# Reordering the casts, masks, products and bursts of a fused retention and leaky-ReLU kernel

## The chip, the cores and the metric

The kernel runs on one core of one Trainium2 chip. The metric is the device time of one execution in microseconds (us). Times of single instructions and stretches come from one profiled execution; they are counted from the start of its span, which is the time from its first to its last instruction.

## The reference

The inputs q, k and v are [8 batches, 8 heads, 576 positions, 64] in float32, w_in is [512, 2048], w_out is [2048, 512]. Each head h has a decay `gamma[h] = 1 - 2**(-5-h)`.

```python
scores = scale * np.matmul(q, k.transpose(0, 1, 3, 2))
Dmat = np.where(rel >= 0, gamma[:, None, None] ** rel[None, :, :], 0.0)   # rel = pos_q - pos_k
x = matmul(scores * Dmat, v)          # retention: causal, decayed, no softmax
x = x.transpose(0, 2, 1, 3).reshape(4608, 512)
h = x @ w_in                          # first layer
g = np.maximum(0.01 * h, h)           # leaky ReLU
out = g @ w_out                       # second layer, [4608, 512] float32
```

## The kernel before, in words

**Units and groups.** The 4608 tokens are cut into 36 units of 128 tokens (two chunks of 64) and into 9 groups of 512 tokens, four units each. A unit goes through retention and gives its slice of `xT`, the transposed input of the first layer. A group then goes through the first layer (`gt`, after the leaky ReLU) and the second.

**One unit of retention.** `load` (L119) brings k, q and v in as float32 (256 KB each). `cast_k` (L170) is a ScalarE copy to f16; `cast_q` (L174) and `cast_v` (L177) multiply by a decay table on VectorE, or on GpSimd from unit 8 on. q and k are transposed: for units 0 to 7 on TensorE (`transpose_pe`, L190, one PSUM buffer of `acc` for each, copied out by `transposed`, L206), from unit 8 on by a DMA (`transpose_dma`, L181). `scores` (L209) makes 16 products of q and k and 16 of k and v, in one PSUM tile `sc` that has a single buffer. On VectorE, `masks` (L231) gives the masked scores `s16`, and `state` (L242) carries the running state from chunk to chunk. `state_cast` (L270) makes it f16 for the outputs. `st_before` (L278) shows who needs which: chunk 1 of a unit needs the state cast of chunk 0, chunk 0 of the next unit that of chunk 1.

**Two forms of the outputs.** `outputs_acc` (L309) sums the near and the far part in PSUM, in two halves with a drain of TensorE between; `x_copy` (L340, ScalarE) then writes `xT`. `outputs` (L283) writes both parts apart, without the drain; `own` (L353, ScalarE) copies the near part and `add` (L359, VectorE) adds the far part into `xT`. The tile `ot` has one buffer too.

**First layer.** The pieces are `h_half` (L394: 256 tokens, two blocks of 128 features, 8 matmuls of 256 columns), `h_unit` (L399 to L407: 128 tokens, four blocks, 16 matmuls of 128 columns) and `h_block` (L389: 512 tokens, one block). Each is followed by a ScalarE leaky ReLU of 128x512. They and the TensorE transposes share the four buffers of `acc`.

**Second layer.** Group 0 uses the plain product (`wide`, L419, 16 calls of 4 matmuls of 512 columns). All others use `seven` (L469), a seven-product scheme whose extra operands come from `mix_weights` (L440) and `mix` (L455) on VectorE.

**The order is written by hand.** The scheduler is in manual mode (L82): every engine runs its instructions in program order. TensorE, VectorE, ScalarE, GpSimd and the SyncE queue are five lists, and the position of a call sets its place in each list that it touches. There are three stages:

- L558 to L606, the start: weights and units 0 to 7 are queued for loading, mostly on the GpSimd queue; units 0 to 3 go through retention, and `keep_warm` (L546) puts matmuls with no use between, 512 columns each.
- L633 to L679, group 0's first layer with units 4 to 7 in between, then group 1's first layer. w_in is loaded in four quarters; quarter n holds the feature blocks of `h_half` pieces 2n and 2n+1.
- L720 to L748, group 0's second layer and group 1's. A `burst` (L686) is the scores of one unit with the outputs of the one before it; `ahead` (L701) casts a later unit and transposes it by DMA. From L750 on, groups 2 to 8 follow in a loop.

Of the kernel before, what the change touches and what calls it, by code (L numbers as in the profile page):

```python
# [18 lines left out]
def kernel(  # L19
# [9 lines left out]
    nc = tc.nc  # L29
# [89 lines left out]
    def load(u, eng=None, after=None):  # L119
        for x in (1, 0, 2):  # L120
            t = ld_pool.tile([P, H, D], FP, name=f"t32_{x}")
            t32[u, x] = t
            c = 2 * u
            same = c % CB + 1 < CB
            e = eng[x] if isinstance(eng, dict) else eng or nc.sync
            engs = e if isinstance(e, tuple) else (e,)
            n = H // len(engs)
            for j, rows in ((0, P),) if same else ((0, CH), (1, CH)):
                b, w = (c + j) // CB, (c + j) % CB
                for i, e in enumerate(engs):  # L130
                    hs = slice(n * i, n * i + n)
                    d = e.dma_start(  # L132
                        out=t[CH * j : CH * j + rows, hs],
                        in_=(q, k, v)[x][b, hs, CH * w : CH * w + rows, :].rearrange(
                            "h t d -> t h d"
                        ),
                    )
                    if after is not None:
                        behind(d, *after)
                        after = None  # L140
                    last_load[u, x] = d

# [63 lines left out]
    def transposed(u, x, copy):  # L206
        copy(out=qkT[u][:, x], in_=tr[u, x])
# [261 lines left out]
    def seven(g, hooks, last=False):  # L469

        r = {}
        s = sums[g]

        def product(name, lhs, rhs, fresh):
            if fresh:
                r[name] = acc_pool.tile([P, 2, HN], FP, name="acc")
            order = (
                [(f, tb) for tb in range(2) for f in range(HF)]
                if last
                else [(f, tb) for f in range(HF) for tb in range(2)]  # L480
            )
            for n, (f, tb) in enumerate(order):
                nc.tensor.matmul(  # L483
                    out=r[name][:, tb, :],
                    lhsT=lhs[:, f, tb * P : (tb + 1) * P],
                    rhs=rhs[:, f, :],
                    start=fresh and n == 0,
                    stop=f == HF - 1,
                    skip_group_check=True,
                )  # L490

        def keep(name, of, plus=None):
            r[name] = m_pool.tile([P, 2, HN], FP, name=name)
            if plus is None:
                nc.scalar.copy(out=r[name], in_=r[of])  # L495
            else:
                nc.vector.tensor_tensor(out=r[name], in0=r[of], in1=r[plus], op=ADD)

        def give(a, b, of, plus=None, parts=1):
            if ("o", a) not in r:  # L500
                r["o", a] = o_pool.tile([P, 2, DM], FP, name="osb")
            for n in range(parts):
                ts = slice(n * 2 // parts, (n + 1) * 2 // parts)
                to = r["o", a][:, ts, b * HN : (b + 1) * HN]
                if plus is None:
                    nc.scalar.copy(out=to, in_=r[of][:, ts])
                else:
# [12 lines left out]
            if r["n", a] == 2 and not (last and a == 1):  # L520
                store(g, a, r["o", a])

        plan = (
            ("p1", g_part(g, 0, 0), w_part(0, 0), True, lambda: keep("k1", "p1")),
            ("p1", g_part(g, 0, 1), w_part(1, 0), False, lambda: give(0, 0, "p1")),
            ("p6", s[:, 1], w_mix[:, 1], True, lambda: keep("u2", "p6", "k1")),
            ("p5", s[:, 0], w_mix[:, 0], True, lambda: keep("v", "p5", "u2")),
            ("p7", g_part(g, 1, 0), w_mix[:, 2], True, lambda: give(1, 1, "p7", "v")),
            ("p5", g_part(g, 0, 0), w_part(1, 1), False, lambda: give(0, 1, "p5", "u2")),
            (  # L530
                "p7", g_part(g, 1, 1), w_mix[:, 3], False,
                lambda: give(1, 0, "p7", "u2", 2 if last else 1),
            ),
        )
        for n, (name, lhs, rhs, fresh, then) in enumerate(plan):
            product(name, lhs, rhs, fresh)
            then()
            if n == 0:
                mix(g, 3, 0)
                mix(g, 3, 1)  # L540
            for f in hooks.get(n, ()):
                f()
# [14 lines left out]

    keep_warm(7)  # L558
    load(0, {1: nc.sync, 0: (nc.sync, nc.gpsimd), 2: nc.gpsimd})
    for u in range(1, 3):  # L560
        load(u, nc.gpsimd)
    load(3, {1: nc.sync, 0: nc.gpsimd, 2: nc.gpsimd})
    for f in range(3):
        load_w_in(f)
    load(4, nc.gpsimd)
    load_w_in(3)
    for u in range(5, 8):
# [4 lines left out]
    cast_k(0)  # L572
    transpose_pe(0, 1)
    transposed(0, 1, act_copy)
    keep_warm(2)
    cast_q(0, nc.vector)
    cast_v(0, nc.vector)
    transpose_pe(0, 0)
    transposed(0, 0, act_copy)
    keep_warm(2)  # L580
    cast_k(1)
    cast_q(1, nc.vector)
    for u in range(4):
# [24 lines left out]

    def halves(g, *items):
        for a, fb in items:  # L610
            h_half(g, a, fb)

    def casts(u, eng):
        cast_k(u)
        cast_q(u, nc.vector)
        cast_v(u, eng)

    def turn(u, x):
        transpose_pe(u, x)
# [13 lines left out]
    halves(0, (0, 0), (0, 1))  # L633
    finish(3)
    halves(0, (0, 2), (0, 3), (1, 0), (1, 1))
    casts(4, nc.vector)
    halves(0, (1, 2), (1, 3))
# [24 lines left out]
    settle(6)  # L662
    casts(7, nc.vector)
    h_unit(5, 1)
    turn(7, 1)
    halves(1, (0, 4))
    finish(6)
    turn(7, 0)
    halves(1, (0, 5))
    scores(7)  # L670
    settle(7)
    halves(1, (0, 6), (0, 7))
    finish(7)
    load(8, after=(w_out_loads[2],))
    load(9)
    for n in range(4):
        mix_weights(n, 0)
        mix_weights(n, 1)
        halves(1, (1, 2 * n), (1, 2 * n + 1))  # L679

    def mixes(g, *ns):
        for n in ns:
            mix(g, n, 0)
# [30 lines left out]
    def step(u):  # L714
# [2 lines left out]
        ahead(u + 2)  # L717


    at = {  # L720
        0: lambda: (ahead(8), load(10)),
        3: lambda: (ahead(9), load(11)),
        6: lambda: (ahead(10), load(12)),
        9: lambda: (burst(8, False), ahead(11), load(13)),
        12: lambda: mixes(1, 0),
        14: lambda: mixes(1, 1),
    }
    for n in range(16):
        wide(n // 4, n % 4)
        if n in at:  # L730
            at[n]()

    def early(u):
        burst(u)
        if u < 12:
            ahead(u + 3)
            load(u + 5)
# [12 lines left out]
    first = [f for i in range(4) for f in (i, i + HF)]  # L750
    second = [f for i in range(4, 8) for f in (i, i + HF)]
# [46 lines left out]
```

## Time and profile before

| | |
|---|---|
| median of 7 runs | 309.41 us (306.39 to 311.15) |
| the profiled execution: its time, its span | 309.41 us, 307.6 us |
| mean granted TensorE clock | 0.967 of full |
| TensorE busy, share of the span | 289.3 us, 94% |
| VectorE, ScalarE, GpSimd | 168.5, 144.2, 104.3 us |
| units 0 to 3, up to the first matmul of the first layer | to 22.4 us |
| first layer of groups 0 and 1, units 4 to 7 | 22.4 to 69.7 us |
| second layer of groups 0 and 1, units 8 to 12 | 69.7 to 102.0 us |
| groups 2 to 8 | 102.0 to 303.6 us |

How to read it: the span is 1.8 us shorter than the execution's own time. "Busy" of TensorE counts a matmul at half clock as busy too, so a full row doesn't say that the array ran at its speed; the granted clock has a row of its own (tenths of full speed). A line of the timeline gives start, length, engine, line, operation, and in brackets the idle time before it and what ended that.

### The profile page before, as it was taken

To read this page: it belongs to the slowest core of one execution; us is meant where nothing else is said; L and a number is where in the kernel's file an instruction comes from. 1 tells how busy PE (TensorE), PEld (TensorE's weight loads), DVE (VectorE), ACT (ScalarE), POOL (GpSimd) and SP (SyncE) were. 2 spreads that over 40 slices of the span, in tenths; PEclk is the share of its full clock that TensorE was granted. 3 is DMA by queue.
4 is the path that set the end of the run, shared out by engine and by line. 5 is a ranking of instruction groups with operands and counts; after the bars stand their busy time and mean duration, and the time that the engine had idled before them with its cause. 6 is when DMAs were issued, how large, how long until landed. Compare 5 with 4: busy or idle time off the path is not lost.

```text
span 307.6 us, 9356 instructions
## 1 busy us (share of the span) xinstructions
PE 289.3 (94%) x4071; PEld 196.2 (64%) x4071; DVE 168.5 (55%) x291; ACT 144.2 (47%) x254; POOL 104.3 (34%) x125
## 2 busy tenths in 40 slices
PE   6799976799989999999999999999999999999994
PEld 2468865684467547854884587468647854784583
DVE  1853456620798347735863575557457736741342
ACT  4546642444232576167417723762476247406610
POOL 8949504100644333523352433333334333000000
PEclk9769997979999999999999999999999999999999
DMA  7999999005999999997759667966896651003003
GB/s 216 266 217 225 279 188 205 3 2 132 211 209 271 173 321 207 204 261 158 159 129 284 148 149 157 273 139 142 221 217 113 139 173 36 4 10 129 0 0 139
DMA packets 131258, 50.01 MB, mean 163 GB/s; under 512 B 120752, under 2 KB 125488, under 8 KB 131216
## 3 DMA queue, kind: packets, MB, share of 16 engines
q1 hardware_dynamic: 124864, 39.46, 56.6%
q0 software_dynamic: 6064, 9.83, 14.3%
q8 instruction: 32, 0.52, 0.7%
q10 hardware_dynamic: 288, 0.11, 0.1%
q14 instruction: 10, 0.08, 0.1%
HBM read 36.81 MB, written 9.44 MB: 150 GB/s over the span
## 4 chain that ended last, share of the span: by engine, by line
PE 79%; DMA 6%; SPq 4%; issue 3%; DVE 3%; POOL 2%; ACT 2%; DVEq 0%; POOLq 0%; ACTq 0%
PE acc L373 40%; PE acc L483 28%; DMA t<-in_q_dram 3%; PE sc L215 2%; SPq L132 2%; DMA qkT<-qk 2%; PE ot L321 2%; SPq L183 1%; PE acc L200 1%; PE sc L224 1%; PE acc L549 1%; DMA t<-in_v_dram 1%; PE ot L291 1%; PE ot L302 1%; POOL t L132 1%
## 5 line engine op out<-in xcount | busy, mean ns | idle before, releaser
L373 PE MATMUL acc<-xT,w_in 128*128 128x512 f16 (+2 forms) x736 | 133.8, 340 | 1.8 <-ACT xT L341 1.4
L387 ACT ACTIVATE gt<-acc 128x512 f16<-128x512 f32 x144 | 85.7, 597 | 58.8 <-PE acc L373 57.3
L373 PEld LDWEIGHTS <-w_in 128*128 128x128 f16 x736 | 69.9, 101 | 54.9 <-issue 2.1
L483 PEld LDWEIGHTS <-gt 128*128 128x128 f16 x640 | 61.8, 98 | 10.3 <-issue 1.2
L233 DVE TENSOR_TENSOR s<-sc,cs 128x512 f16<-128x512 f32 x36 | 24.7, 685 | 49.2 <-PE sc L224 49.2
L483 PE MATMUL acc<-w_out,gt 128*128 128x256 f16 x384 | 45.9, 273 | 1.2 <-ACT k L495 1.0
L175 POOL TENSOR_TENSOR qk<-t,cs 128x512 f16<-128x512 f32 x28 | 29.4, 1050 | 42.5 <-DMA t<-in_q_dram 40.9
L273 POOL CAST st<-s 128x512 f16<-128x512 f32 x21 | 12.8, 609 | 85.7 <-DVE s L257 55.8
L355 ACT COPY own<-ot 128x512 f32<-128x512 f32 x28 | 16.4, 586 | 35.0 <-PE ot L302 27.5
L179 POOL TENSOR_TENSOR v<-t,cs 128x512 f16<-128x512 f32 x28 | 31.9, 1139 | 0.5 <-DMA t<-in_v_dram 0.5
L172 ACT CAST qk<-t 128x512 f16<-128x512 f32 x36 | 22.3, 620 | 17.8 <-DMA t<-in_k_dram 12.6
L483 PE MATMUL acc<-w_mix,gt 128*128 128x256 f16 x256 | 30.6, 273 | 0.0
L467 DVE TENSOR_TENSOR mix<-gt 128x1024 f16<-128x1024 f16 x16 | 14.2, 891 | 28.8 <-ACT gt L387 28.8
L483 PE MATMUL acc<-w_mix,mix 128*128 128x256 f16 x256 | 29.4, 273 | 0.0
L483 PEld LDWEIGHTS <-mix 128*128 128x128 f16 x256 | 25.0, 98 | 2.9
L257 DVE TENSOR_TENSOR s<-sc,s 128x256 f32<-128x256 f32 x40 | 16.8, 420 | 6.1 <-PE sc L224 5.6
L360 DVE TENSOR_TENSOR xT<-ot,own 128x512 f16<-128x512 f32 x28 | 19.1, 683 | 1.6 <-ACT own L355 1.6
L215 PEld LDWEIGHTS <-qkT 64*64 64x64 f16 x576 | 7.9, 110 | 12.9 <-issue 10.2
L467 DVE TENSOR_TENSOR mix<-mix,gt 128x1024 f16<-128x1024 f16 x16 | 14.8, 932 | 0.5
L508 DVE TENSOR_TENSOR osb<-acc,u 128x512 f32<-128x512 f32 (+1 forms) x17 | 11.0, 655 | 7.5 <-PE acc L483 7.5
L423 PE MATMUL acc<-w_out,gt 128*128 128x512 f16 x64 | 14.2, 380 | 0.0
L276 POOL CAST st<-s 128x256 f16<-128x256 f32 x7 | 3.2, 454 | 30.2 <-DVE s L261 18.7
(52 smaller groups left out, 246.6 us busy)
## 6 DMA issues: line engine op xcount, KB each, us to landing
out_dram<-osb SPq DMA_DIRECT2D x17, 512.0 KB, 4.0
t<-in_k_dram SPq DMA_DIRECT2D x27, 256.0 KB, 3.8
t<-in_q_dram SPq DMA_DIRECT2D x25, 256.0 KB, 4.4
t<-in_v_dram SPq DMA_DIRECT2D x25, 256.0 KB, 4.5
w_in<-in_moe_w_in_dram POOLq DMA_DIRECT2D x8, 256.0 KB, 6.9
w_out<-in_moe_w_out_dram POOLq DMA_DIRECT2D x4, 512.0 KB, 10.1
t<-in_v_dram POOLq DMA_DIRECT2D x7, 256.0 KB, 5.6
t<-in_q_dram POOLq DMA_DIRECT2D x6, 256.0 KB, 5.8
```

The source lines that it names most:

```text
L172: nc.scalar.copy(out=qk16[u][:, 1], in_=t32[u, 1])
L175: eng.tensor_tensor(out=qk16[u][:, 0], in0=t32[u, 0], in1=decay(u, 0), op=MUL)
L179: eng.tensor_tensor(out=v16[u], in0=t32[u, 2], in1=decay(u, 1), op=MUL)
L233: nc.vector.tensor_tensor(out=s16s[u], in0=sc_tiles[u][:, :, 0], in1=mask_sb.unsqueeze(1).unsqueeze(1).to_broadcast([P, 2, NP, CH]), op=MUL,)
L257: nc.vector.tensor_tensor(out=to, in0=st, in1=carry[0], op=ADD)
L355: nc.scalar.copy(out=owns[u], in_=ot_tiles[u][:, :, 0:NP].rearrange("q j c t -> q c j t"))
L360: nc.vector.tensor_tensor(out=x_of(u).rearrange("q (c g) t -> q c g t", g=2), in0=ot_tiles[u][:, :, NP : 2 * NP].rearrange("q g (c j) t -> ...
L373: nc.tensor.matmul(out=hps[:, n, :], lhsT=w_in16[:, c, f * P : (f + 1) * P], rhs=xT[g][:, c, ts], start=(c == 0), stop=(c == NP - 1),)
L387: nc.scalar.activation(out=out, in_=in_, func=mybir.ActivationFunctionType.Lrelu)
L423: nc.tensor.matmul(out=ys[tb], lhsT=g_t[0][:, f, tb * P : (tb + 1) * P], rhs=w_out16[:, f, :], start=(f == 0), stop=(f == NF - 1),)
L467: nc.vector.tensor_tensor(out=z[:, fs], in0=a[:, fs], in1=b[:, fs], op=op)
L483: nc.tensor.matmul(out=r[name][:, tb, :], lhsT=lhs[:, f, tb * P : (tb + 1) * P], rhs=rhs[:, f, :], start=fresh and n == 0, stop=f == HF - ...
```

## The change

In the start, k of unit 1 is loaded by the SyncE queue and k of unit 3 only after it has landed; the GpSimd queue loses one load, and takes the cast of v of unit 3 between the second and the third quarter of w_in. On VectorE, the mask of unit 0 stands ahead of the casts of q and v of unit 1. There are 29 instead of 23 `keep_warm` matmuls. The outputs of unit 0 stand ahead of the q transpose of unit 1, and two pieces of the first layer stand around the outputs of unit 2.

In the first layer, each cast of k stands earlier on ScalarE, ahead of the state cast that it followed, and the state cast of chunk 1 stands behind the unit's outputs. Units 3 to 6 use `outputs`, `own` and `add` (called `finish2`) in place of `outputs_acc` and `x_copy`. Two `h_unit` pieces (units 6 and 7) replace two `h_half` pieces right after the outputs of unit 7. The pieces of group 0 come in another order. `ahead(8)` with `load(10)` and `ahead(9)` with `load(11)` move from group 0's second layer into group 1's first layer.

In the second layers, bursts 8, 9 and 10 stand at pieces 4 and 9 of `wide` and after its end (before: burst 8 at piece 9, burst 9 after the end), and two bursts instead of three stand inside group 1's `seven`. In the last group, the product p6 is placed between the two products of p1.

```diff
-                    if after is not None:
-                        behind(d, *after)
+                    if after is not None and (x in after or not isinstance(after, dict)):
+                        behind(d, *(after[x] if isinstance(after, dict) else after))
                         after = None
...
+        if last:
+            plan = (plan[0], plan[2], plan[1]) + plan[3:]
...
-    for u in range(1, 3):
-        load(u, nc.gpsimd)
-    load(3, {1: nc.sync, 0: nc.gpsimd, 2: nc.gpsimd})
-    for f in range(3):
-        load_w_in(f)
+    load(1, {1: nc.sync, 0: nc.gpsimd, 2: nc.gpsimd})
+    load(2, nc.gpsimd)
+    load(3, {1: nc.sync, 0: nc.gpsimd, 2: nc.gpsimd}, {1: (last_load[1, 1],)})
+    load_w_in(0)
+    load_w_in(1)
+    cast_v(3, nc.gpsimd)
+    load_w_in(2)
     load(4, nc.gpsimd)
...
-    keep_warm(2)
+    keep_warm(3)
...
-    keep_warm(2)
+    keep_warm(3)
     cast_k(1)
-    cast_q(1, nc.vector)
     for u in range(4):
         n = u + 1
         scores(u)
+        if not u:
+            keep_warm(3)
         state(u, 0)
         state_cast(u, dve_copy, (0,))
         masks(u)
-        if n == 1:
+        if not u:
+            cast_q(1, nc.vector)
             cast_v(1, nc.vector)
         state(u, 1)
         if n < 4:
             transpose_pe(n, 1)
+            transposed(n, 1, act_copy)
+            if not u:
+                keep_warm(3)
+                outputs_acc(0)
+                x_copy(0)
+                keep_warm(1)
             transpose_pe(n, 0)
-            transposed(n, 1, act_copy)
             transposed(n, 0, act_copy)
-            keep_warm(3)
+            keep_warm(3 if u == 1 else 2)
         if n < 3:
             cast_k(n + 1)
             cast_q(n + 1, nc.vector)
+        if n < 2:
             cast_v(n + 1, nc.vector)
         state_cast(u, act_copy, (1,))
-        if n < 4:
-            outputs_acc(u)
-            x_copy(u)
-            keep_warm(1)
+        if u == 1:
+            outputs_acc(1)
+            x_copy(1)
+            keep_warm(2)
+        elif u == 2:
+            h_half(0, 0, 0)
+            outputs_acc(2)
+            x_copy(2)
+            h_half(0, 0, 1)
...
         masks(u)
         state(u, 1)
-        state_cast(u, act_copy, (1,))
 
     def finish(u):
         outputs_acc(u)
         x_copy(u)
+        state_cast(u, act_copy, (1,))
+
+    def finish2(u):
+        outputs(u)
+        own(u)
+        add(u)
+
+    halves(0, (0, 2), (0, 3))
+    finish2(3)
+    halves(0, (0, 4), (0, 5), (1, 0))
+    cast_k(4)
+    cast_qv(4)
+    halves(0, (1, 1), (1, 2), (1, 3))
     turn(4, 1)
-    halves(0, (0, 4), (0, 5))
+    halves(0, (1, 4))
     turn(4, 0)
-    halves(0, (1, 4))
-    casts(5, nc.vector)
-    halves(0, (1, 5))
+    halves(0, (1, 5), (0, 6))
+    cast_k(5)
     scores(4)
     settle(4)
-    halves(0, (0, 6), (0, 7))
-    finish(4)
+    cast_qv(5)
+    halves(0, (0, 7), (1, 6))
+    finish2(4)
+    state_cast(4, act_copy, (1,))
     turn(5, 1)
-    halves(0, (1, 6))
+    cast_k(6)
+    halves(0, (1, 7))
     turn(5, 0)
-    halves(0, (1, 7))
     scores(5)
     settle(5)
-    casts(6, nc.vector)
+    cast_qv(6)
     h_unit(4, 0)
     turn(6, 1)
+    cast_k(7)
     h_unit(4, 1)
-    finish(5)
+    finish2(5)
+    state_cast(5, act_copy, (1,))
     turn(6, 0)
     h_unit(5, 0)
     scores(6)
     settle(6)
-    casts(7, nc.vector)
+    cast_qv(7)
...
     halves(1, (0, 6), (0, 7))
     finish(7)
...
+    load(8, after=(w_out_loads[2],))
+    load(9)
+    h_unit(6, 0)
+    mix_weights(0, 0)
+    mix_weights(0, 1)
+    h_unit(7, 0)
+    for n in range(1, 4):
+        mix_weights(n, 0)
+        mix_weights(n, 1)
+        halves(1, (1, 2 * n))
+        if n < 3:
+            ahead(7 + n)
+            load(9 + n)
+        halves(1, (1, 2 * n + 1))
...
     at = {
-        0: lambda: (ahead(8), load(10)),
-        3: lambda: (ahead(9), load(11)),
-        6: lambda: (ahead(10), load(12)),
-        9: lambda: (burst(8, False), ahead(11), load(13)),
-        12: lambda: mixes(1, 0),
-        14: lambda: mixes(1, 1),
+        1: lambda: (ahead(10), load(12)),
+        4: lambda: (burst(8, False), ahead(11), load(13)),
+        9: lambda: early(9),
+        11: lambda: mixes(1, 0),
+        13: lambda: mixes(1, 1),
     }
...
-    early(9)
+    early(10)
     mixes(1, 2)
-    seven(
-        1,
-        {
-            0: [lambda: early(10)],
-            2: [lambda: early(11)],
-            4: [lambda: early(12)],
-        },
-    )
+    seven(1, {0: [lambda: early(11)], 4: [lambda: early(12)]})
```

More of the change, by code (lines that the diff above doesn't have):

```diff
@@ L611, in halves, with cast_qv @@
             h_half(g, a, fb)
-    def casts(u, eng):
-        cast_k(u)
+    def cast_qv(u):
         cast_q(u, nc.vector)
-        cast_v(u, eng)
+        cast_v(u, nc.vector)
     def turn(u, x):
@@ L631, in finish @@
         x_copy(u)
[L633 to L637, printed above, removed]
+        state_cast(u, act_copy, (1,))
[9 more added lines that the diff above has]
+    halves(0, (1, 1), (1, 2), (1, 3))
     turn(4, 1)
-    halves(0, (0, 4), (0, 5))
+    halves(0, (1, 4))
     turn(4, 0)
-    halves(0, (1, 4))
-    casts(5, nc.vector)
-    halves(0, (1, 5))
+    halves(0, (1, 5), (0, 6))
+    cast_k(5)
     scores(4)
     settle(4)
-    halves(0, (0, 6), (0, 7))
-    finish(4)
+    cast_qv(5)
+    halves(0, (0, 7), (1, 6))
+    finish2(4)
+    state_cast(4, act_copy, (1,))
     turn(5, 1)
-    halves(0, (1, 6))
+    cast_k(6)
+    halves(0, (1, 7))
     turn(5, 0)
-    halves(0, (1, 7))
     scores(5)
     settle(5)
-    casts(6, nc.vector)
+    cast_qv(6)
     h_unit(4, 0)
     turn(6, 1)
+    cast_k(7)
     h_unit(4, 1)
-    finish(5)
+    finish2(5)
+    state_cast(5, act_copy, (1,))
     turn(6, 0)
@@ L666 @@
     halves(1, (0, 4))
-    finish(6)
+    finish2(6)
+    state_cast(6, act_copy, (1,))
     turn(7, 0)
@@ L673 @@
     finish(7)
[L674 to L679, printed above, removed]
     def mixes(g, *ns):
@@ L717, in step, with early @@
         ahead(u + 2)
-    at = {
-        0: lambda: (ahead(8), load(10)),
-        3: lambda: (ahead(9), load(11)),
-        6: lambda: (ahead(10), load(12)),
-        9: lambda: (burst(8, False), ahead(11), load(13)),
-        12: lambda: mixes(1, 0),
-        14: lambda: mixes(1, 1),
+    load(8, after=(w_out_loads[2],))
[12 more added lines that the diff above has]
+        halves(1, (1, 2 * n + 1))
+    def early(u, out=True):
+        burst(u, out)
+        if 8 < u < 12:
+            ahead(u + 3)
+            load(u + 5)
+    at = {
+        1: lambda: (ahead(10), load(12)),
[3 more added lines that the diff above has]
+        13: lambda: mixes(1, 1),
     }
@@ L731 @@
             at[n]()
[L733 to L737, printed above, removed]
-    early(9)
-    mixes(1, 2)
-    seven(
-        1,
-        {
-            0: [lambda: early(10)],
-            2: [lambda: early(11)],
-            4: [lambda: early(12)],
-        },
-    )
+    early(10)
+    mixes(1, 2)
+    seven(1, {0: [lambda: early(11)], 4: [lambda: early(12)]})
     first = [f for i in range(4) for f in (i, i + HF)]
```

## The prediction

> **What bounds the kernel now.** I read the page first: TensorE is busy for 94% of the span, and over slices of 7.7 us its granted clock falls below 9 tenths only in slices 2, 3, 7 and 9.
>
> ```profile
> PE 289.3 (94%) x4071; PEld 196.2 (64%) x4071; DVE 168.5 (55%) x291; ACT 144.2 (47%) x254; POOL 104.3 (34%) x125
> PEclk9769997979999999999999999999999999999999
> ```
>
> So TensorE's own list is the bound, and only idle time or half clock on it can be won. The table by stretches says where: from 102 to 276 us TensorE is busy for 173.74 of 174.00 us at full clock, while the change touches nothing there. From 69.7 to 102 it is busy for 29.95 of 32.30. The rest lies before 69.7. The waits of TensorE, longest in total first:
>
> ```profile
> PE acc L200 <- ACT qk L172: 5.0, 4, 2.3
> PE acc L373 <- ACT xT L341: 1.4, 1, 1.4
> ...
> PE sc L215 <- DVE stmp L260: 1.2, 1, 1.2
> ...
> PE acc L483 <- ACT k L495: 1.0, 2, 0.7
> ```
>
> The k transposes wait for ScalarE's k cast. TensorE's timeline places the three long waits of the first layer, and ScalarE's shows what stood before two of the casts:
>
> ```profile
> 43.01 0.40 PE L200 MATMUL acc<-ident,qk 128*128 128x128 f16 x4 [1.87 <-ACT qk L172]
> 51.73 0.60 PE L200 MATMUL acc<-ident,qk 128*128 128x128 f16 x4 [2.34 <-ACT qk L172]
> 61.02 8.81 PE L373 MATMUL acc<-xT,w_in 128*128 128x256 f16 x64 [1.38 <-ACT xT L341]
> ```
> ```profile
> 42.03 0.40 ACT L276 CAST st<-s 128x256 f16<-128x256 f32 x1 [1.63 <-DVE s L257]
> 42.34 0.61 ACT L172 CAST qk<-t 128x512 f16<-128x512 f32 x1
> ```
>
> k of unit 6 had been issued at 26.56 and landed 6.8 us later, at 33.4; its cast waited 9 us behind a state cast. Each wait also brings a stretch of half clock. By stretches:
>
> ```profile
> 44.94:48.36 3.42, 3.29 (x69) 2.80 (x64) 0.42 (x1) 1.08 (x2) 0.00 (x0) 0.50 0.86 182
> 48.36:51.77 3.41, 1.07 (x21) 0.90 (x18) 3.18 (x7) 1.12 (x4) 2.13 (x2) 1.00 0.98 224
> 51.77:55.19 3.42, 3.33 (x44) 2.42 (x44) 1.27 (x2) 0.99 (x2) 2.44 (x3) 0.50 0.40 88
> 62.01:65.42 3.41, 3.41 (x19) 2.41 (x17) 1.50 (x3) 1.19 (x2) 0.00 (x0) 0.50 0.00 0
> ```
>
> First columns: length, TensorE busy; third from the end: clock. Three stretches of 3.41 us at half clock cost up to 1.7 us each. A fourth, 10.81 to 21.05, lies in the start.
>
> [...]switches at 10.81, 21.05, 44.94, 48.36, 51.77, 55.19, 62.01 and 65.42 lie on one grid of 3.413 us. [...]1.38 us of wait in one grid step (58.60 to 62.01, busy 1.95) was enough. [...]v's cast takes 0.69 us alone and 1.53 at 51.18, beside a GpSimd cast of 1.52.
>
> **The change part by part.** I follow TensorE's list through the new order with the old durations at full clock: an `h_half` or `h_unit` piece 0.875 us, four transposes 0.22, scores 0.38, `outputs` 0.37 (84.33 to 84.70), `outputs_acc` 0.8 to 0.9, a `keep_warm` matmul 0.22 (0.43 at half clock). On the others: casts of q and v and masks 0.60 back to back (0.68 alone), state 0.42 or twice that, state casts 0.30 to 0.41, ScalarE's leaky ReLU, `own`, `x_copy` and k cast 0.6, `add` 0.68.
>
> *Start.* I compare at one point: all of units 0 to 3 and six pieces done. Before: `outputs_acc(3)` ends at 25.12, four more pieces would give 28.6. After: v of unit 0 still lands at 7.8, so the first scores end at 8.86. With the mask first, the outputs of unit 0 can run at 10.45 instead of 11.53. At full clock the chain of VectorE and TensorE then puts the scores of units 1, 2 and 3 at 12.5, 16.0 and 20.0 (before 13.1, 17.8, 22.0). Scores of unit 3 end at 20.35; state, cast, mask and state take VectorE 2.3, then ScalarE 0.4 for the state cast, 1.2 for two leaky ReLUs behind it and 0.6 for `own`, VectorE 0.65 for `add`: piece (1,0) starts at 25.5. If the clock stays at half from 10.8 to 21 as now, the six extra fillers cost 0.43 each and the scores of unit 3 end at 25, so (1,0) starts at 30.1. Between them I take 26.5, near the warm end, since the fillers stand where TensorE was idle (its waits sum to 3.3 us between 1.19 and 11.53). Worth -2.1 (from -3.1 to +1.5). The k load that waits on SyncE has only unit 8 behind it, due at 44 us. GpSimd's v cast waits for v (landed at 14.2) and holds back the third quarter of w_in, issued at 12.5 before, to some 15.4. Its two loads landed at 21.7 and 23.0, behind four others still under way, so they should land no later; (0,4) needs them at 22.5 to 23.0. If that cover is gone, it costs 1 us for each us.
>
> *First layer, from (1,0) to the end of the scores of unit 7.* Before: 28.62 to 56.83, 28.2. After, work: 12 `h_half` and 4 `h_unit` pieces 14.0, eight transposes 1.8, four scores 1.5, three `outputs` 1.1, together 18.4. Waits that remain or are new: scores 5 right after its q transpose must await the VectorE copy, 0.6; `own` and `add` of unit 5 come behind a leaky ReLU on ScalarE and two casts and a copy on VectorE, while `h_unit(5,0)` needs the result, 1.45 (before 0.4 behind `x_copy`); q transpose of unit 7 0.45; scores 7 behind `add(6)` and the copy 0.9. Sum 22.0 with rounding. The 1.45 leaves a grid step about 57% busy, so I charge one drop, 1.7: 23.7, worth -4.5 (from -6.2 to -2.8 with none or two). This holds the gain of the k casts: k of units 5, 6 and 7 land at 30.2, 33.4 and 35.6, and ScalarE comes to their casts at about 33, 35.5 and 38.5. All ScalarE instructions behind such a cast would wait with it, then the leaky ReLUs, then the four `acc` buffers.
>
> *From there to the end of group 1's first layer.* Before 12.84 (56.83 to 69.67). After: two pieces 1.75, `outputs_acc(7)` 0.8, two `h_unit` pieces 1.75 that hide `x_copy(7)`, six pieces 5.25: 9.55. The 1.38 wait and its half clock go. Worth -3.3; without that cover it is -0.2.
>
> *Second layers of groups 0 and 1.* Before 32.33. After: 64 matmuls of 512 columns (14.0) and 112 of 256 (12.25), with five bursts of scores and `outputs` (3.3): 29.5. VectorE is the risk: its mixes took 2.97 for two beside GpSimd's casts (1.48 alone), and `mix(1,1)` now ends right at burst 10. I find 1.0 us of wait at burst 11 for `sc` and the state cast, and 0.7 in small ones: 31.2, worth -1.1 (from -2.5 to +0.5). DMA: transposes 8 and 9 with loads 10 and 11 are issued from about 56 us instead of 71, into what was 54 to 72 us of almost no transfer; the DMA engines were busy for all of 72 to 102, so this adds slack.
>
> *Last group.* p6 in place of the wait of 0.72 for the copy k1; its operand is ready at 292.55, p6's fifth matmul would ask at 292.49. Worth -0.6.
>
> Sum: -2.1 - 4.5 - 3.3 - 1.1 - 0.6 = -11.6. The profiled execution's own time is 309.41 (span 307.6, 1.8 around it), equal to the median, so 309.4 - 11.6 = 297.8 us.
>
> **Rivals.** (a) The waits move rather than go: the start stays cold and the `own`/`add` chains bring two or three drops. For it: VectorE now carries `add` four times in the densest stretch (3.18 of 3.41 us busy at 48.36 to 51.77). Against: the new gaps are smaller than 1.87 and 2.34. Time: +1.5, -2.8, -3.3, +0.5, -0.6 is -4.7, 304.7; halfway 301 to 302. (b) All stays warm: -3.1 - 6.2 - 3.3 - 1.7 (without the small waits) - 0.6 = -14.9, 294.5; if the new waits don't come either, 291.5. (c) Slower: GpSimd's queue behind the v cast. All of w_in's second half, units 4 to 7 and w_out are issued behind it. For it: at 13 to 23 us that queue already waits for landings. Against: it has four loads ahead then. At a landing of the third quarter at about 34.5 instead of 23.0 the gain is gone, at 38 the kernel is 1% slower (312.5). (d) It doesn't do what it says: k lands late once casts come early, ScalarE blocks, and the waits return under the name of a DMA; with slacks of 2 to 3 us I expect little: 306 to 309.
>
> **How the numbers follow.** Likeliest 0.50 (294.5 to 300), (a) 0.30 (300 to 305), (b)'s lower part 0.09 (291 to 294.5), (c) 0.04, (d) 0.07. From 292 to 304.5 leaves out about 2 in 10. Faster by over 1% (below 306.3) is the first three with a little of (d): 0.90; within 1% 0.06; slower 0.04. About 1% is what a measurement of this kernel can tell from no change.
>
> **What would show it.** Right: no wait of `acc L200` on `qk L172` over 0.5 us after 30 us; group 2's first block at about 91 us instead of 102.0; 174 us from there to 276's counterpart unchanged; one or two half-clock stretches before 60 us; no wait of 0.7 on L495. Wrong: `h_unit(5,0)` without a wait on `xT` (my 1.45 is too much), w_in landing after 23 us with TensorE waiting on it, half clock up to 21 us again, or waits of ScalarE's L172 on a DMA.

## The result and the profile after

The changed kernel takes 294.64 us (median of 11 runs, 294.08 to 297.51), the kernel before 308.14 us (28 runs, 305.28 to 311.15). The ratio is 0.9586, with a 95% interval of 0.9553 to 0.9619. Medians here take in all runs; ratios leave out the slow ones, which are those over 1.5% above the fastest of the same kernel. The profiled execution took 295.62 us, 1.0 more than the median, with a span of 293.8 us, 13.8 less than the span shown before. My 297.8 was 3.2 us too high: 1.9 in the gain (11.6 forecast, 13.5 by the medians) and 1.3 in the base (309.4 instead of 308.14).

From the page after: TensorE's busy time and its granted clock in slices of 7.3 us.

```profile
PE 281.3 (96%) x4101; PEld 190.9 (65%) x4101; DVE 172.6 (59%) x294; ACT 144.2 (49%) x254; POOL 105.2 (36%) x125
PEclk9999999999999999999999999999999999999999
```

TensorE runs 30 instructions more and is busy 8 us less, and no slice falls under nine tenths of the clock. The waits of TensorE after, longest in total first:

```profile
PE acc L373 <- issue: 1.4, 1, 1.4
PE sc L215 <- DVE qkT L207: 1.3, 2, 0.7
...
PE acc L373 <- DVE xT L360: 1.2, 1, 1.2
PE acc L373 <- ACT qkT L207: 1.0, 1, 1.0
...
PE acc L200 <- ACT qk L172: 0.2, 1, 0.2
```

The 5.0 us behind ScalarE's k casts are down to 0.2. What is new stands in TensorE's timeline:

```profile
17.81 1.03 PE L373 MATMUL acc<-xT,w_in 128*128 128x256 f16 x8 [0.96 <-ACT qkT L207]
23.25 0.94 PE L373 MATMUL acc<-xT,w_in 128*128 128x256 f16 x7
25.61 4.65 PE L373 MATMUL acc<-xT,w_in 128*128 128x256 f16 x41 [1.42 <-issue]
38.10 0.32 PE L215 MATMUL sc<-qkT 64*64 64x64 f16 x16 [0.75 <-DVE qkT L207]
42.55 1.05 PE L373 MATMUL acc<-xT,w_in 128*128 128x128 f16 x16 [1.18 <-DVE xT L360]
```

The first line is put down to a copy that had ended at 17.08; the second load of w_in's first quarter was issued at 9.9 and landed some 7.8 us later, at 17.7; that is the last thing I find which the piece needs. The third is a pause inside a piece: seven matmuls at 23.25, then the eighth 1.42 us later. The last two were foreseen: the copy ahead of the scores of unit 5 (0.6 forecast, 0.75 measured) and `add` ahead of unit 5's piece (1.45 forecast, 1.18 measured). ScalarE shows the k cast of unit 6 behind a state cast again, but this one is ready:

```profile
36.08 0.58 ACT L355 COPY own<-ot 128x512 f32<-128x512 f32 x1
36.55 0.42 ACT L276 CAST st<-s 128x256 f16<-128x256 f32 x1
36.85 0.63 ACT L172 CAST qk<-t 128x512 f16<-128x512 f32 x1
```

Last the stretches (length, busy time of TensorE, its weight loads, VectorE, ScalarE and GpSimd, clock, DMA share, GB/s): end of the first layer, second layers of groups 0 and 1, and the loop.

```profile
49.08:59.03 9.95, 9.78 (x140) 8.64 (x130) 9.31 (x12) 7.08 (x13) 4.84 (x4) 1.00 0.52 118
59.03:89.13 30.10, 29.68 (x466) 19.62 (x464) 21.10 (x33) 9.28 (x16) 14.68 (x15) 1.00 1.04 223
89.13:263.55 174.42, 174.22 (x2563) 115.80 (x2560) 104.69 (x175) 88.18 (x153) 56.19 (x65) 1.00 0.74 164
```

Group 2's first block begins at 89.13 instead of 102.00. From there to the first block of group 8 it takes 174.42 us, where the kernel before took 174.49 (102.00 to 276.49): the loop is as it was. From that block to the end of the span it is 30.25 after and 31.11 before.

### The profile page after: what moved, and what is told of

Same layout as the page of the kernel before. It is cut to its first block, busy times and chain, and to the rows that moved or that the text cites. A ratio compares the mean times of both kernels' runs of the same rounds, so it can differ in the third digit from the quotient of the medians.

```text
span 293.8 us, 9414 instructions
## 1 busy us (share of the span) xinstructions
PE 281.3 (96%) x4101; PEld 190.9 (65%) x4101; DVE 172.6 (59%) x294; ACT 144.2 (49%) x254; POOL 105.2 (36%) x125
## 4 chain that ended last, share of the span: by engine, by line
PE 85%; DVE 7%; issue 2%; POOL 2%; DMA 2%; ACT 1%; DVEq 0%; POOLq 0%
PE acc L373 41%; PE acc L483 33%; PE acc L423 3%; PE sc L215 3%; POOL t L132 2%; DMA t<-in_v_dram 2%; PE sc L224 1%; DVE mix L467 1%; PE ot L291 1%; DVE s L233 1%; PE ot L302 1%; DVE xT L360 1%; DVE s L257 1%; PE ot L321 1%; DVE qkT L207 1%
## 5 line engine op out<-in xcount | busy, mean ns | idle before, releaser
L373 PE MATMUL acc<-xT,w_in 128*128 128x512 f16 (+2 forms) x752 | 130.9, 330 | 3.6 <-issue 1.4
L373 PEld LDWEIGHTS <-w_in 128*128 128x128 f16 x752 | 67.8, 98 | 55.9 <-issue 4.4
L233 DVE TENSOR_TENSOR s<-sc,cs 128x512 f16<-128x512 f32 x36 | 24.7, 686 | 44.0 <-PE sc L224 44.0
L175 POOL TENSOR_TENSOR qk<-t,cs 128x512 f16<-128x512 f32 x28 | 30.1, 1075 | 22.6 <-PE sc L224 14.2
L355 ACT COPY own<-ot 128x512 f32<-128x512 f32 x32 | 18.7, 585 | 38.8 <-PE ot L302 31.6
L179 POOL TENSOR_TENSOR v<-t,cs 128x512 f16<-128x512 f32 x29 | 33.2, 1146 | 4.3 <-DMA t<-in_v_dram 3.5
L467 DVE TENSOR_TENSOR mix<-gt 128x1024 f16<-128x1024 f16 x16 | 14.9, 936 | 28.8 <-ACT gt L387 28.8
L483 PE MATMUL acc<-w_mix,mix 128*128 128x256 f16 x256 | 29.6, 273 | 0.0
L360 DVE TENSOR_TENSOR xT<-ot,own 128x512 f16<-128x512 f32 x32 | 21.9, 684 | 3.0 <-ACT own L355 3.0
L467 DVE TENSOR_TENSOR mix<-mix,gt 128x1024 f16<-128x1024 f16 x16 | 14.0, 879 | 0.5
```

Source lines behind the costliest of these rows:

```text
L175: eng.tensor_tensor(out=qk16[u][:, 0], in0=t32[u, 0], in1=decay(u, 0), op=MUL)
L179: eng.tensor_tensor(out=v16[u], in0=t32[u, 2], in1=decay(u, 1), op=MUL)
L233: nc.vector.tensor_tensor(out=s16s[u], in0=sc_tiles[u][:, :, 0], in1=mask_sb.unsqueeze(1).unsqueeze(1).to_broadcast([P, 2, NP, CH]), op=MUL,)
L355: nc.scalar.copy(out=owns[u], in_=ot_tiles[u][:, :, 0:NP].rearrange("q j c t -> q c j t"))
L360: nc.vector.tensor_tensor(out=x_of(u).rearrange("q (c g) t -> q c g t", g=2), in0=ot_tiles[u][:, :, NP : 2 * NP].rearrange("q g (c j) t -> ...
L373: nc.tensor.matmul(out=hps[:, n, :], lhsT=w_in16[:, c, f * P : (f + 1) * P], rhs=xT[g][:, c, ts], start=(c == 0), stop=(c == NP - 1),)
```

## The experiments

Twelve runs in three sets of four, each set on another chip. The kernel before was timed beside each set; its median was 306.64, 307.54 and 307.90 us. "Changed kernel" stands for the 294.64 above, or for 294.28 in the third set, where it ran again. Differences "more" or "less" are of medians. Across sets they are rough: in the first set the kernel before was faster and its ratios have intervals of up to 0.02, so that fewer fillers, for one, are 0.5 us slower than the changed kernel by the medians and 2.4 by the ratios (0.9665 against 0.9586). Where two sets differ by less than 2 or 3 us, the profiles have to decide.

### The k casts put back

```diff
-    cast_k(5)      # and those of units 6 and 7, from their earlier places
     scores(4)
     settle(4)
+    state_cast(4, act_copy, (1,))      # and those of units 5 and 6
+    cast_k(5)
     cast_qv(5)
...
     finish2(4)
-    state_cast(4, act_copy, (1,))
```

> The changed kernel with the k casts of units 5, 6 and 7 put back behind the state casts of the unit before, and those state casts back ahead of the outputs; all else as changed. Theory (k casts free TensorE's list): the two long waits of the k transposes of units 6 and 7 come back, 1.5 to 2.3 us each, and at least one of them brings a half-clock step of 1.7, so 3.5 to 6 us slower than the changed kernel (ratio to before about 0.97 to 0.978). Rival (VectorE's chain of own, add and casts bounds this stretch anyway, so the waits overlap with those that are there): under 1.5 us slower, ratio under 0.964.

Measured: 300.44 us, ratio 0.9852 (0.9767 to 0.9938), 5.8 us more than the changed kernel. TensorE's timeline and the clock:

```profile
40.12 0.61 PE L200 MATMUL acc<-ident,qk 128*128 128x128 f16 x4 [1.81 <-ACT qk L172]
49.12 0.40 PE L200 MATMUL acc<-ident,qk 128*128 128x128 f16 x4 [2.22 <-ACT qk L172]
```
```profile
PEclk9999978999999999999999999999999999999999
```

Both waits are back, and the clock falls in slices 6 and 7 (some 37 to 52 us), where TensorE waits. The rival falls: VectorE's chain does not hide them. The ratio lies above the expected 0.978; part of that is the faster kernel before of this set.

### The k casts alone

```diff
-    settle(u): ... state(u, 1); state_cast(u, act_copy, (1,))
+    settle(u): ... state(u, 1)          # state cast behind x_copy, units 4 to 7
+    cast_k(5)   # after piece (1,4);  cast_k(6) after turn(5, 1);  cast_k(7) after turn(6, 1)
```

> The kernel before with one edit: the k casts of units 5, 6 and 7 earlier on ScalarE and the state casts of units 4 to 7 behind the outputs. Theory (k casts are the largest single part and stand alone): the waits of 1.87 and 2.34 us go, with one or two half-clock steps, so 4 to 6 us faster than before (ratio 0.980 to 0.987), while the wait of 1.38 for unit 7's copy stays. Rival (they only pay together with the other forms of outputs and the new order): under 2 us, ratio over 0.993.

Measured: 300.26 us, ratio 0.9733 (0.9671 to 0.9795), 7.3 us less than before: more than expected, and over half of the whole gain, from the casts of k and the state casts that change places with them. TensorE's timeline of this kernel:

```profile
52.18 7.15 PE L373 MATMUL acc<-xT,w_in 128*128 128x256 f16 x64 [0.67 <-ACT xT L341]
59.16 8.80 PE L423 MATMUL acc<-w_out,gt 128*128 128x512 f16 x40
...
83.08 0.32 PE L215 MATMUL sc<-qkT 64*64 64x64 f16 x16 [2.15 <-DMA qkT<-qk]
89.38 0.32 PE L215 MATMUL sc<-qkT 64*64 64x64 f16 x16 [1.89 <-DMA qkT<-qk]
93.53 4.48 PE L373 MATMUL acc<-xT,w_in 128*128 128x512 f16 x20
```

The second layer begins at 59.16, where the changed kernel has 59.03: up to there, in these two executions, this edit alone brings as much as all of them. The changed kernel has new waits on this way that the other lacks, 0.96, 1.42 and 1.18 us among them. But the second layers then take 34.4 us (59.16 to 93.53) against 30.1, with 4.0 us of wait for DMA transposes. Whether the earlier k casts cause these waits is not shown: the second profile of the kernel before, further down, has 3.6 us of them although its second layers begin at 65.93.

The clock of this profile reads full throughout, yet its start ran at half clock. Three fillers take 1.49 us at first and 0.81 later:

```profile
PEclk9999999999999999999999999999999999999999
```
```profile
10.38 1.49 PE L549 MATMUL acc<-idle 128*128 128x512 f16 x3
18.49 0.81 PE L549 MATMUL acc<-idle 128*128 128x512 f16 x3
```

Four transposes take 0.61 us at 6.88 too, and 0.39 at 29.16. So the clock of a page, and the mean clock of a run, can miss half clock in the start.

### The old second layers

```diff
-    ahead(8), load(10), ahead(9), load(11) inside group 1's first layer; bursts 8, 9 at pieces 4, 9
-    early(10); ...; seven(1, {0: early(11), 4: early(12)})
+    0: (ahead(8), load(10)), 3: (ahead(9), load(11)), 6: ..., 9: (burst(8, False), ...)
+    early(9); ...; seven(1, {0: early(10), 2: early(11), 4: early(12)})
```

> The changed kernel with the second layers of groups 0 and 1 as before: units 8 and 9 cast and transposed inside group 0's second layer, burst 8 at piece 9, three bursts inside the seven products. Theory: the 2.2 us that this stretch gained (32.3 to 30.1) come back, from waits of VectorE's backlog at the third burst, so 1.7 to 2.5 us slower than the changed kernel. Rival (the loads come earlier now in any case, so the order no longer matters): under 0.7 us.

Measured: 297.93 us, ratio 0.9680 (0.9623 to 0.9737), 3.3 us more than the changed kernel, above the expected range. By landmarks the same: 58.05 to 91.42 is 33.4 us against 30.1. Its three waits:

```profile
80.75 0.32 PE L215 MATMUL sc<-qkT 64*64 64x64 f16 x16 [1.43 <-DVE stmp L260]
81.72 0.32 PE L291 MATMUL ot<-s,v 64*64 64x64 f16 x16 [0.53 <-DVE xT L360]
87.27 0.32 PE L215 MATMUL sc<-qkT 64*64 64x64 f16 x16 [1.50 <-DMA qkT<-qk]
```

The first two are the backlog of VectorE that the kernel before had too (1.2 and 0.5); the third is the transpose of unit 12. The first profile of before had no wait for a transpose there; the second one, shown below with p6 alone, awaited two, 1.41 and 2.23 us, and its second layers took 34.0 us (65.93 to 99.95) instead of 32.3. So the rival falls. The edit puts back both the `ahead` calls and the places of the bursts; what each is worth alone is not shown.

### The start and its fillers

```diff
     # fewer fillers: 2, 2 instead of 3, 3; none behind scores(0) and T(1, k)
     # old start: loads, casts and order of units 0 to 3 as before, pieces (0,0), (0,1) behind
```

> The changed kernel without eight of the filler matmuls of the start (those that the change added ahead of the first first-layer piece: one, one, three and three). Theory (the fillers hold the clock through the start): half clock returns for two or three steps of 3.41 us between 7 and 21 us, the first first-layer piece starts 0.5 to 3 us later than at 17.8 and the kernel is 1 to 3 us slower (ratio 0.962 to 0.969). Rival (the order of casts and masks alone closes the gaps, or w_in's landing at 17.7 sets the first piece in any case): same time within 0.5 us, first piece at 17.8. The pause of 1.42 us inside a piece at 25.6 should stand about 16 TensorE instructions later in the list if it is a fetch of instructions, and at the same instruction if it is a data wait.

> The changed kernel with the whole start of before (loads, casts, fillers, order of units 0 to 3, two first-layer pieces after the start). Theory: the start gives 2 us of the gain, so 2 us slower than the changed kernel (ratio 0.965), with half clock from about 11 to 21 us. Rival (w_in and the loads bound the first layer, so a slow start is caught up): within 0.7 us.

Measured: fewer fillers 295.12 us (ratio 0.9665, 0.9596 to 0.9733), old start 295.76 us (0.9679, 0.9599 to 0.9759): 0.5 and 1.1 us more than the changed kernel. With fewer fillers the clock is at half for two steps, from 9.7 to 16.6 us, and the first piece starts at 18.66 instead of 17.81:

```profile
PEclk9689999999999999999999999999999999999999
```
```profile
18.66 1.04 PE L373 MATMUL acc<-xT,w_in 128*128 128x256 f16 x8
...
24.10 1.92 PE L373 MATMUL acc<-xT,w_in 128*128 128x256 f16 x16
26.82 3.44 PE L373 MATMUL acc<-xT,w_in 128*128 128x256 f16 x30 [0.80 <-DVE xT L360]
```

So without these eight fillers two steps ran at half clock, where the changed kernel's clock was full. But all but 0.2 us of the delay is gone by 26.82, where (1,0) awaits `add(3)`: in the changed kernel (1,0) starts at 26.6, behind the pause. The old start, at half clock from 9.1 to 15.9, gave its first piece at 20.61 and a second layer at 59.32 against 59.03. The forecast of 2 us for the start seemed too large; the third set takes this up. The pause itself is not to be seen with fewer fillers, at no instruction.

### Outputs in the old form

```diff
     def finish2(u):
-        outputs(u); own(u); add(u)
+        outputs_acc(u); x_copy(u)
```

> The changed kernel with outputs_acc and x_copy for units 3 to 6 in place of outputs, own and add. Theory (the form without a drain saves 0.43 us of TensorE four times, but its add costs the wait of 1.18 before unit 5's piece and parts of two others): the two nearly cancel, within 1 us of the changed kernel (ratio 0.956 to 0.962). Rival 1 (the outputs form is a main source of the gain): 1.5 to 3 us slower. Rival 2 (the add chain costs more than it saves): 1 us or more faster.

Measured: 293.90 us, ratio 0.9641 (0.9545 to 0.9737), 0.7 us less than the changed kernel by the medians and 1.7 more by the ratios. The profiles say that the two forms nearly cancel. From the first piece to the second layer it took 40.5 us (17.21 to 57.73), the changed kernel 41.2, of which 0.56 is its longer pause. By the estimate above the form without the drain saves TensorE some 1.7 us (four times 0.43, the difference of 0.8 and 0.37 us in the first profile). It pays them back in waits: 1.18, 0.75, 0.59 and 0.39 us between 37 and 49 us in the changed kernel, where this one has 0.52 and 0.34.

### No cover for unit 7's copy, and p6 alone

```diff
-    h_unit(6, 0); ...; h_unit(7, 0)
+    halves(1, (1, 0)); ...; halves(1, (1, 1))
```

> The changed kernel with the two half pieces right behind unit 7's outputs again, which need unit 7, in place of the two pieces of units 6 and 7. Theory: TensorE waits about 0.9 us for x_copy of unit 7 there; if the wait brings a half-clock step, 2.5 us slower than the changed kernel, if not, 0.9 us. Rival (the wait of before was long because ScalarE's state cast and two leaky ReLUs stood ahead of the copy, and these are gone): under 0.5 us.

Measured: 295.77 us, ratio 0.9600 (0.9545 to 0.9656), 1.1 us more than the changed kernel by the medians, 0.4 by the ratios. The profile shows a wait of 0.67 us for `x_copy` at 52.25, and no half clock. The first theory had the mechanism, with 0.9 for the wait; the time alone cannot tell 0.5 from 0.9.

```diff
+        if last:
+            plan = (plan[0], plan[2], plan[1]) + plan[3:]      # on the kernel before
```

> The kernel before with one edit: p6 between the two products of p1 in the last group. Theory: the wait of 0.72 us for k1 goes and nothing else changes, 0.6 to 0.9 us faster, which is below what the times of this kernel can tell; the profile shows it. Its profile is also a second look at the start and the first layer of before: if the half-clock stretches depend on the phase of the clock's grid, their places and number differ from the first look, while the waits of 1.87, 2.34 and 1.38 stay.

Measured: 306.52 us, ratio 0.9984 (0.9948 to 1.0020), no difference that the times show. From group 2's first block to the end it takes 204.75 us (99.95 to 304.7), the kernel before 205.6, the changed kernel 204.67. The wait for k1 is gone; in its place the 16 matmuls on the mixed weights take 2.04 us instead of 1.91:

```profile
289.93 2.04 PE L483 MATMUL acc<-w_mix,mix 128*128 128x256 f16 x16
291.81 1.91 PE L483 MATMUL acc<-w_out,gt 128*128 128x256 f16 x16
```

This is also a second profile of the start and the first layer of before. Its clock:

```profile
PEclk9599997799999999999999999999999999999999
```

The waits of 1.87 and 2.35 are there as in the first profile; the one of 1.38 is 0.67 here, against the expectation. And half clock runs from 9.1 to 15.9 and from 50.0 to 56.9 (two grid steps each), not from 10.8 to 21.1, 44.9 to 48.4, 51.8 to 55.2 and 62.0 to 65.4, and the span is 304.7 instead of 307.6. So the profile on which I forecast was one with much half clock.

The wait of 1.87 brought none this time. Its grid step and the next one, here:

```profile
39.77:43.18 3.41, 1.89 (x50) 1.69 (x52) 1.99 (x5) 2.02 (x4) 0.00 (x0) 1.00 1.22 199
43.18:46.59 3.41, 2.96 (x82) 2.48 (x74) 1.33 (x4) 1.18 (x2) 0.00 (x0) 1.00 1.10 188
```

TensorE was busy for 1.89 us of that step. In the first profile, steps with 1.84 (41.53 to 44.94) and 1.95 (58.60 to 62.01) were followed by half clock. Nor did half clock follow the transposes' waits of 1.41 and 2.23 here, or those of 2.15 and 1.89 with the k casts alone. So the forecast's "each wait also brings a stretch of half clock" does not hold in general, and these runs do not settle what decides it.

### The start once more, and two attempts at a better kernel

```diff
     # acc and turn:     outputs_acc, x_copy for units 3 to 6; turn(5, 0) ahead of piece (1, 7)
     # w_in first:       and load_w_in(0) ahead of load(3); cast_v(3) behind load_w_in(2)
     # acc, old start:   the first of these, with the whole start of before
     # change again:     the changed kernel, unaltered
```

> The changed kernel with outputs_acc and x_copy for units 3 to 6 (as in the run that had these alone) and the q transpose of unit 5 ahead of the last half piece of group 0, so that its copy is covered. Theory (the waits of TensorE for add and for the copy are all that the new form costs): the waits of 1.18, 0.75 and 0.59 are gone, 1 to 2 us faster than the changed kernel run beside it. Rival (outputs_acc's drain gives it back): within 0.5 us.

> The run with outputs_acc and the earlier transpose, and also the first quarter of w_in ahead of q and v of unit 3 on the GpSimd queue, and GpSimd's cast of v of unit 3 behind the third quarter. Theory (the first piece waits for w_in's landing at 17.7): the first piece starts at about 16.8 and the kernel is another 0.5 to 1 us faster. Rival (unit 3 comes late instead, or the pause inside a piece at about 25 us takes it up): within 0.4 us.

> The changed kernel once more, unaltered, as the measure beside the three others of this call: about 294.6 us, and if the pause of 1.42 us inside a piece of the first layer belongs to the place in TensorE's list, it is there again after the seventh matmul of that piece.

> The run with outputs_acc and the earlier transpose, but with the whole start of before. With the changed kernel's own first layer the old start cost only 0.3 to 1.1 us, while my sum said 2.1. If the waits for add hid the difference, the old start is 1.5 to 2.5 us slower here than the run without it. If the start itself is worth little, because w_in and the pause in the list set the pace of the first pieces, it is under 1 us slower.

Measured in one set: changed kernel again 294.28 us (ratio 0.9577, 0.9534 to 0.9621), acc and turn 293.17 (0.9550, 0.9503 to 0.9597), w_in first 299.03 (0.9651, 0.9582 to 0.9720), acc with the old start 295.98 (0.9657, 0.9599 to 0.9714).

*Acc and turn* is 1.1 us under the changed kernel, at the low end of what I expected; five of its six times (292.49 to 293.71) lie below five of the other's six (293.85 to 294.88), but the intervals of the ratios overlap. It is the best of all kernels here by its median. The waits of 1.18, 0.75 and 0.59 are gone; 0.34 for `x_copy` remains.

*Old start with acc* costs 2.8 us against *acc and turn*, more than I expected, and the intervals of these two just fail to overlap. So by the times the start is worth about what I forecast. Why it is more here than the 1.1 before is argued, not shown: the pause and the late `add(3)` can have hidden a part in the changed kernel. The profiles of these two differ by only 0.7 us of span (292.6 and 291.9), and this execution of the old start ran at full clock from 4.7 us on and was the fastest of its six. What made the others slower, up to 298.52, is not shown.

*W_in first* is slower than *acc and turn* by 0.0101 of the kernel before, some 3 us. The rival is right in kind, unit 3 comes late, and it costs far more than the 0.4 us that it allowed. The page's clock and the lines of TensorE, ScalarE and GpSimd:

```profile
18.65 0.62 PE L200 MATMUL acc<-ident,qk 128*128 128x128 f16 x8 [2.96 <-ACT qk L172]
```
```profile
17.97 0.62 ACT L172 CAST qk<-t 128x512 f16<-128x512 f32 x1 [4.13 <-DMA t<-in_k_dram]
```
```profile
18.24 1.14 POOL L179 TENSOR_TENSOR v<-t,cs 128x512 f16<-128x512 f32 x1 [5.19 <-DMA t<-in_v_dram]
```
```profile
PEclk9987999999999999999999999999999999999999
```

With two loads of w_in ahead of q and v of unit 3, k of unit 3 comes late as well, though it is on the other queue and its issue there had ended at 7.8 us, as in *acc and turn*; how the loads delay it is not shown. Its cast starts at 17.97 instead of 13.97, the k transpose waits 2.96 us, and half clock follows (8 and 7 tenths in the slices from 14.8 to 29.6 us). ScalarE kept to the order of its list, so this is rival (d) of the forecast, at another place: a k cast that waits for its load, with 4.13 us of idle time ahead of it, holds up what stands behind it on ScalarE, here a state cast that ran at 15.30 in *acc and turn* and runs at 18.50.

*The changed kernel again* missed my expectation on the pause. The first piece started at 16.62, as w_in's first quarter landed over a microsecond sooner, and TensorE then waited for w_in's third quarter; no pause followed:

```profile
22.99 5.45 PE L373 MATMUL acc<-xT,w_in 128*128 128x256 f16 x48 [0.85 <-DMA w_in<-in_moe_w_in_dram]
```

## Why the prediction was right, step by step

The time lies in the range, on its low side. The largest step, the k casts, came as forecast and is shown by experiments. In the start and at the end of the first layer the sum is right for another reason, and that is luck. By its own steps (spans, us; the loop gives another -0.1):

| step | forecast | changed kernel's profile | the experiments |
|---|---|---|---|
| start, to piece (1,0) | -2.1 | -2.0 (28.6 to 26.6) | 1.1; 2.8 with the old outputs |
| (1,0) to the scores of unit 7 | -4.5 | -5.7 (28.2 to 22.5) | k casts back: +5.8 |
| to the end of the first layer | -3.3 | -2.9 (12.84 to 9.95) | cover alone: 0.67 of wait |
| second layers of groups 0 and 1 | -1.1 | -2.2 (32.3 to 30.1) | old order: +3.3 |
| last group | -0.6 | -0.9 (31.1 to 30.2) | p6 alone: -0.85 |
| sum | -11.6 | -13.8 | |

**K casts: right, shown from both sides.** Put back they cost 5.8 us, alone they bring 7.3, and the long waits come and go with them.

**The clock: mis-sized.** I charged one half-clock step, 1.7 us, because the wait for `add` would leave a grid step 57% busy, as the step of 58.60 to 62.01 had been (1.95 of 3.41 us), which half clock followed. It did wait, 1.18 us, and no half-clock step followed in any of six profiles with that wait (the changed kernel twice, without cover, the old second layers, fewer fillers, the old start; 1.18 or 1.19 us each). After the first 6 us no half clock came before 290 us, where I had expected one or two stretches before 60. That term is most of what was missing in the second row: 22.0 without it, against 22.5 measured. The other side of it is the kernel before. In 26 of its executions, those beside the first two sets, the mean granted clock runs from 0.956 to 0.997 and the time from 303.56 to 312.27 us; a straight line through them (correlation -0.57) gives 1.4 us for each 0.01 and 304.7 at full clock. From this estimate some 10 us of the gain would be waits and order, and about 3.4 clock. It is a weak estimate: the line explains a third of the spread, the mean clock can miss half clock in the start, and it counts half clock after the last matmul (all that the changed kernel's 0.998 lacks, from 292.84 on). In the two profiled executions TensorE's busy time alone differs by 8.0 us, for 30 instructions more. So the split between clock and waits stays open. The changed kernel's runs have 0.994 to 1.000 and spread by 3.4 us. Half clock in the start differs between the two profiles of before as well: 10.24 us in the first, 6.83 in the second.

**The start: right in size by luck.** I put 26.5 between a warm and a cold chain. The clock stayed full, as in my warm chain (25.5), but w_in's first quarter landed at 17.7 instead of 17.0 as in the profile before (0.96 of wait), and the pause took 1.42; I had neither. In the second execution, without both, (1,0) starts at 24.7, which makes this step -3.9. The cover that I named for w_in's third quarter was as thin as said: in the second execution TensorE waited 0.85 us for it.

**The end of the first layer: right in size, wrong cause.** I gave nearly all of the 3.3 us to the cover of unit 7's copy and said that 0.2 remains without it. Without the cover the stretch takes 10.5 us (48.76 to 59.23) against 9.95 with it, so it is worth some 0.5. The rest of the gain is the half clock and half of the wait of 1.38, and both belonged to one execution: in the second profile of before, without any cover, the wait is 0.67 and no half clock follows it.

**The second layers: right sign, too small.** I foresaw 1.0 us at burst 11 and 0.7 in small waits; one wait of 0.42 came. What I treated as slack was worth more: the old order runs into the DMA transposes in three of its four profiles (1.5 us of wait on the changed kernel, 4.0 with the k casts alone, 3.6 with p6 alone). The gain of this step therefore depends on the others, and on the execution of before that it is held against: 2.2 us against its first profile, 3.9 against its second, 3.3 against the old order on the changed kernel. That VectorE's mixes stretch beside GpSimd's casts came as forecast. A pair of weight mixes took 2.98 us beside them, a pair of the same form 1.28 us with GpSimd idle:

```profile
53.17 2.98 DVE L448 TENSOR_TENSOR w_mix<-w_out,w_mix 128x1024 f16<-128x1024 f16 x2
57.28 1.28 DVE L448 TENSOR_TENSOR w_mix<-w_out,w_mix 128x1024 f16<-128x1024 f16 x2
```

GpSimd cast q and v of unit 9 from 52.84 to 55.60. Nothing waited for these mixes.

**The rivals.** (a), waits that move to `own` and `add`, was true in kind: 0.75, 1.18 and 0.59 us; *acc and turn* shows that they cost about 1 us. (c), GpSimd's queue, did not come in its size: v of unit 3 was cast at 14.11, as its load landed, and the wait for w_in's third quarter was 0 in one execution and 0.85 us in the other. (b), all warm, is what happened, 294.5 in the forecast; that the time agrees to 0.1 us is luck, since its gain of 14.9 was 1.4 too large and its base 1.3 too high.

## What to carry to other kernels

An engine that works through one list for two chains should run the instruction whose input is ready long before first: here three casts, moved past a state cast, were worth half of a 13.5 us gain. When one stage becomes faster, look at what feeds the next: with that edit alone TensorE waited 4.0 us for the transposes behind it. A wait of TensorE can cost more than its length, as half clock may follow (it did after waits of 1.38, 1.87 and 2.34 us in the first profile of before); but it is no fixed charge, since waits of up to 2.23 us passed here without. A profile with half clock is one draw among several, so take a second one before pricing it, and compare the length of like instructions, not the clock row alone.

## What I had not expected

- **A pause inside a piece.** In five profiles (the changed kernel, without cover, old second layers, old outputs, acc and turn) TensorE stops for 0.4 to 1.4 us inside piece (0,4), behind the seventh matmul, or behind the sixth where `outputs_acc` has put one drain more into the list. No data wait is shown. In a sixth (acc with the old start) it stops for 0.64 us at another place, behind seven of eight matmuls of unit 2's outputs (18.94 us). Before that stop 443 matmuls and weight loads are recorded, before the changed kernel's 696, so the places are 253 apart. A packet of the instruction queue moves 1.2 to 2.2 us before each of the six (at 23.0 us in the changed kernel), but also at 22.4 us with fewer fillers, where no pause follows. The page after counts 32 packets and 0.52 MB on that queue, some 16 KB each. That TensorE stops for such a packet, held up by other transfers, is a guess of mine and not shown: with nearly the same list and the k casts put back at most 0.3 us shows (16 matmuls in 2.21 us instead of 1.92), and with the same list it was absent when TensorE had just waited 0.85 us for w_in.
- **Landings move by a microsecond** between executions of one kernel: the first piece of the changed kernel started at 17.81 and at 16.62, which changes which of the waits behind it is seen.
